# A pool of their own for the staging tiles of q, and the normalising multiply placed between the mask multiplies on VectorE

## The chip, the cores and the metric

The kernel runs on one core of a Trainium2 chip. The metric is the device time of one execution in microseconds (us), lower is better; here the executions of one kernel within one set of rounds lie within 0.26% of each other. TensorE is called PE in the profile (PEld is its weight load), VectorE DVE, ScalarE ACT, GpSimd POOL, and SyncE, which issues the DMA transfers here, SP. A "verdict" of faster or slower takes 2%.

## The reference

Two layers, each an attention block and a token-mixing MLP, with a layer norm and a residual sum around each. Only the attention matters here: every query looks at 8 keys, at distances 0, 2, ..., 14.

```python
def _A_ref(x, wqkv, wo):                      # x: 1 x 2048 x 1024, bf16
    H = 32; Dh = D // H; W, dil = 8, 2
    q, k, v = ...                             # x @ wqkv, 32 heads of 32
    idx = pos[:, None] - (jnp.arange(W) * dil)[None, :]
    mask = idx >= 0
    logits = einsum("bhsd,bhswd->bhsw", q, k[idx]) * scale
    attn = softmax(where(mask, logits, -1e9))
    return einsum("bhsw,bhswd->bhsd", attn, v[idx]).reshape(B, S, D) @ wo
x = x + _A_ref(layernorm(x), A_wqkv, A_wo)
x = x + _B_ref(layernorm(x), ...)             # MLP over the tokens, 2048 -> 3584 -> 2048
# the same two lines once more
```

## The kernel before

The attention runs in 32 *visits* per layer. A visit computes scores of four heads for half of the even or of the odd tokens (512 queries), then the values of the visit before it, then two 512-column pieces of the next q or k projection. Even visits (b = 0) project q, odd visits (b = 1) project k. The parts that the change touches:

```python
x2p = pool("x2p", 6)      # six tiles in turn: residual loads xr, sums xn, reciprocals rd, q staging qs (and others)
pcp = pool("pcp", 2)
psa = pool("psa", 1, space=bass.MemoryType.PSUM)     # acc: ONE buffer
# ...
def qk_chunk(u, wts, part, n):                # 8 matmuls into ps
    # ...
    if part:
        nc.scalar.copy(out=kT[u % 2][:, ls], in_=ps[:])
    else:
        qs = x2("qs", [P, 512])
        nc.scalar.copy(out=qs[:], in_=ps[:])
        for h in range(HG):                   # 4 q copies, 32 partitions each: head h from partition 32*h
            hp = slice(h * DH, (h + 1) * DH)
            nc.vector.tensor_copy(out=qB[u % 2][hp, h, ls], in_=qs[hp, :])

def scores(u, b):
    # ... 16 matmuls into ss
    nc.scalar.activation(out=pc[:]..., in_=ss[...], func=ACT.Exp, ...)
    for r in range(P // KG):                  # masks 0, 1, 2, 3: 32 partitions each, mask r from partition 32*r
        rp = slice(r * KG, (r + 1) * KG)
        nc.vector.tensor_tensor(out=Pm[rp, ...], in0=pc[rp], in1=mk, op=ALU.mult)

def values(u, b, v, oT):
    acc = a_tile()
    # if b: 4 tiny matmuls on the block before (8 columns)      -> "values, first line" (L404)
    # 16 matmuls on this block: need all four masks             -> "values, second line" (L408)
    # matmuls with ones: the sums of the softmax
    nc.scalar.activation(out=rd[:], in_=acc[:, 1, :], func=ACT.Ln)
    nc.scalar.activation(out=rd[:], in_=rd[:], func=ACT.Exp, scale=-1.0)
    nc.vector.tensor_tensor(out=oT[g][...], in0=acc[:, 0, :], in1=rd[:], op=ALU.mult)   # "normalise"

def out_proj(c, i, oT, wo, res, dst, h2):
    xr = x2("xr")
    nc.sync.dma_start(out=xr[:], in_=res(c, i))                    # residual load
    # per half: 8 matmuls, then xn = ps + xr on VectorE, which frees the PSUM tile ps
    nc.sync.dma_start(out=rows(dst, c, i), in_=xn[:])              # store
    # ...

for vis in range(2 * NU):
    # ...
    in_order(scores, u, b)
    if vis:
        in_order(values, *divmod(vis - 1, 2), v, oT)
    for n in range(2):
        if u + 1 < NU:
            in_order(qk_chunk, u + 1, wts, *chunks[2 * b + n])
        else:
            in_order(out_proj, 0, 2 * b + n, oT, wo, res, xa[li], h2)
```

The first line of values runs only for b = 1, that is, in the *even* visit that follows.

The softmax here doesn't subtract the row's maximum and nothing guards it: scores larger than these inputs give would overflow.

## Time and profile before

| | before |
|---|---|
| time, median (range) | 1304.88 us (1304.62 to 1305.46, 3 runs); 1305.1 us with the 3 runs beside the changed kernel |
| span of the profiled run | 1303.6 us, granted clock 1.00 |
| PE, DVE, ACT busy | 98%, 35%, 29% |
| PE idle behind the residual add | 7.3 us |

From the page: the line of busy times (microseconds, share of the span, instructions), then the chain of waits that ended last, as shares of the span by engine.

```profile
PE 1278.7 (98%) x8258; PEld 592.9 (45%) x8414; DVE 454.4 (35%) x971; ACT 372.4 (29%) x628; POOL 2.4 (0%) x15
...
PE 95%; DMA 2%; DVE 2%; issue 1%; ACT 1%; DVEq 0%; SPq 0%
```

TensorE bounds the kernel, and VectorE is hardly on the chain. The waits view for PE (who waited for whom: total us, times, longest):

```profile
PE m L448 <- DVE xn L450: 7.3, 6, 2.0
PE m L352 <- issue: 4.6, 29, 0.2
```

The second line needs no cause: some matmul records are missing from the trace (963 of 1024 in this group).

The timeline of one pair of visits in layer 1. Columns: start, duration (of the whole merged group), engine, line, operation, out<-in, shapes, count, and in brackets the idle time ahead of it. L380 is scores, L383 the exponential, L388 the masks, L425 the end of the reciprocal, L427 the normalise, L362 the q copies, L404 and L408 the values.

```profile
152.58 0.46 PE L380 MATMUL s<-qB,kT 128*32 128x160 bf16 x16
...
154.00 2.02 DVE L388 TENSOR_TENSOR Pm<-pc,band 32x640 bf16<-32x640 bf16 x4 [1.14 <-ACT pc L383]
154.48 0.63 ACT L425 ACTIVATE rd<-rd 128x512 f32<-128x512 f32 x1
...
156.06 0.69 DVE L427 TENSOR_TENSOR oT<-acc,rd 128x512 bf16<-128x512 f32 x1
156.66 2.38 DVE L362 COPY qB<-qs 32x512 bf16<-32x512 bf16 x8
...
157.07 0.46 PE L380 MATMUL s<-qB,kT 128*32 128x160 bf16 x16
...
157.36 0.41 PE L408 MATMUL acc<-Pm,v 128*32 128x136 bf16 x16
...
159.07 2.03 DVE L388 TENSOR_TENSOR Pm<-pc,band 32x640 bf16<-32x640 bf16 x4
...
161.13 0.69 DVE L427 TENSOR_TENSOR oT<-acc,rd 128x512 bf16<-128x512 f32 x1
...
161.48 0.46 PE L380 MATMUL s<-qB,kT 128*32 128x160 bf16 x16
...
161.88 0.19 PE L404 MATMUL acc<-Pm,v 128*32 128x8 bf16 x4
...
161.90 0.42 PE L408 MATMUL acc<-Pm,v 128*32 128x136 bf16 x16
```

Two things are to be seen. First, VectorE works with gaps of 0.05 us at most from 154.00 to 161.82 (161.13 + 0.69), 7.82 us of the 8.90 us between the two even visits. Second, PE waits for the end of that chain although no idle time is listed. In the odd visit values start 0.29 us after the scores (157.36 - 157.07); in the even visit they start 0.40 us after (161.88 - 161.48), which is 0.06 us after the normalise ended. Recorded matmuls overlap: in the odd visit the scores end at 157.53, 0.17 us after the start of values. In the even visit their recorded end, 161.94, is 0.06 us after the start of values, and so it covers the wait.

### The profile page before, as it was taken

Reading aid. Unit: us, or ns where it says so; the run is one execution under the profiler, and the core shown is the slowest. Engines: PE = TensorE matmul, PEld = TensorE weight load, DVE = VectorE, ACT = ScalarE, POOL = GpSimd, SP = SyncE. Lnnn points to the kernel's source line nnn. Section 1 sums busy time; section 2 is a strip of 40 time slices with the busy share of each in tenths; the row PEclk is TensorE's granted clock in tenths of the full one; section 3 lists DMA queues with packets and bytes.
Section 4 is the critical chain, followed back from the end, with each engine's and each line's share of the span. In section 5 each row is a group of like instructions: output and inputs, shape, how many; then the busy total and the mean of one; then the engine's idle time right before and its main releaser. Section 6 shows DMA issues by size and latency. Waiting matters only on the chain.

```text
span 1303.6 us, 19189 instructions
## 1 busy us (share of the span) xinstructions
PE 1278.7 (98%) x8258; PEld 592.9 (45%) x8414; DVE 454.4 (35%) x971; ACT 372.4 (29%) x628; POOL 2.4 (0%) x15
## 2 busy tenths in 40 slices
PE   9999999999999999999999999999999999999998
PEld 4444444444444444444444444444444444444443
DVE  7468888820000013322300788888000000111111
ACT  5356665431111110000023666654211111000000
POOL 0000000000000000000000000000000000000000
PEclk9999999999999999999999999999999999999999
DMA  8620113452223236465432101034522222334330
GB/s 236 134 76 18 34 34 105 139 154 82 80 65 88 60 94 153 123 153 146 129 81 64 35 23 29 18 130 155 145 65 81 81 60 73 109 105 137 113 92 32
DMA packets 195812, 121.58 MB, mean 93 GB/s; under 512 B 37904, under 2 KB 177424, under 8 KB 195728
## 3 DMA queue, kind: packets, MB, share of 16 engines
q1 hardware_dynamic: 195728, 120.36, 32.6%
q8 instruction: 65, 1.06, 0.3%
q14 instruction: 19, 0.16, 0.0%
HBM read 96.48 MB, written 16.78 MB: 87 GB/s over the span
## 4 chain that ended last, share of the span: by engine, by line
PE 95%; DMA 2%; DVE 2%; issue 1%; ACT 1%; DVEq 0%; SPq 0%
PE m L352 17%; PE s L518 15%; PE s L475 15%; PE acc L475 7%; PE m L475 7%; PE m L518 7%; PE acc L518 7%; PE m L448 6%; PE m L337 4%; PE m L255 4%; PE s L380 2%; PE acc L408 1%; DMA xr<-in_A_x_dram 1%; PE acc L412 1%; DMA xr<-xb 1%
## 5 line engine op out<-in xcount | busy, mean ns | idle before, releaser
L518 PEld LDWEIGHTS <-w 128*128 128x128 bf16 x1792 | 175.3, 98 | 211.4
L475 PEld LDWEIGHTS <-w 128*128 128x128 bf16 x1792 | 175.3, 98 | 211.4
L352 PE MATMUL m<-hT,wqk 128*128 128x512 bf16 x963 | 223.4, 379 | 6.2 <-issue 4.6
L521 DVE SCALAR_TENSOR_TENSOR xo<-s,b_sb,xs 128x512 bf16<-128x512 f32 x32 | 24.0, 751 | 539.8 <-PE s L518 533.5
L475 PE MATMUL s<-h,w 128*128 128x512 bf16 x878 | 201.3, 379 | 0.8
L518 PE MATMUL s<-g,w 128*128 128x512 bf16 x884 | 199.3, 379 | 0.7
L352 PEld LDWEIGHTS <-wqk 128*128 128x128 bf16 x1024 | 95.2, 98 | 118.0 <-issue 10.7
L388 DVE TENSOR_TENSOR Pm<-pc,band 32x640 bf16<-32x640 bf16 x256 | 123.7, 483 | 46.0 <-ACT pc L383 39.2
L448 PE MATMUL m<-wo,oT 128*128 128x512 bf16 x500 | 111.9, 379 | 7.9 <-DVE xn L450 7.3
L475 PE MATMUL acc<-h,w 128*128 128x512 bf16 x440 | 103.1, 379 | 0.5
L518 PE MATMUL acc<-g,w 128*128 128x512 bf16 x436 | 99.7, 379 | 0.5
L362 DVE COPY qB<-qs 32x512 bf16<-32x512 bf16 x256 | 72.6, 284 | 77.5 <-ACT qs L359 73.4
L475 PE MATMUL m<-h,w 128*128 128x512 bf16 x438 | 98.5, 379 | 0.5
L518 PE MATMUL m<-g,w 128*128 128x512 bf16 x436 | 98.3, 379 | 0.6
L174 ACT ACTIVATE ln<-mv,eps 128x1 f32<-128x1 f32 x64 | 18.9, 295 | 244.2 <-DVE mv L182 238.8
L448 PEld LDWEIGHTS <-oT 128*128 128x128 bf16 x512 | 49.6, 98 | 68.6 <-issue 10.3
L482 ACT ACTIVATE g<-s,b_sb 128x1024 bf16<-128x1024 f32 x28 | 31.2, 1113 | 166.1 <-PE s L475 154.3
L255 PE MATMUL m<-wv,hT 128*128 128x512 bf16 x250 | 55.6, 379 | 1.0 <-ACT hT L249 0.7
L337 PE MATMUL m<-wv,hT 128*128 128x512 bf16 x251 | 55.2, 379 | 0.3
L359 ACT CAST qs<-m 128x512 bf16<-128x512 f32 x64 | 37.5, 585 | 51.4 <-PE m L352 50.3
L383 ACT ACTIVATE pc<-s,shift 128x640 bf16<-128x640 f32 x64 | 51.1, 799 | 0.0
L356 ACT CAST kT<-m 128x512 bf16<-128x512 f32 x64 | 37.5, 585 | 46.5 <-PE m L352 46.5
(57 smaller groups left out, 677.3 us busy)
## 6 DMA issues: line engine op xcount, KB each, us to landing
w<-in_B_w_dram SPq DMA_DIRECT2D x56, 512.0 KB, 3.8
w<-in_B_w_dram SPq DMA_DIRECT2D x64, 448.0 KB, 4.6
wqk<-in_A_wqkv_dram SPq DMA_DIRECT2D x16, 512.0 KB, 5.7
xa<-xn SPq DMA_DIRECT2D x32, 256.0 KB, 2.0
xs<-xa SPq DMA_DIRECT2D x32, 256.0 KB, 3.3
wv<-in_A_wqkv_dram SPq DMA_DIRECT2D x8, 512.0 KB, 5.2
wo<-in_A_wo_dram SPq DMA_DIRECT2D x8, 512.0 KB, 4.0
xr<-in_A_x_dram SPq DMA_DIRECT2D x16, 256.0 KB, 3.2
```

The costliest lines, as they stand in the source:

```text
L255: r = nc.tensor.matmul(pss_[k, n][:], lhsT=hT[:, kt, cols(*order[k])], rhs=wv[n][kt // 4][:, kt % 4, :], start=(kt == 0), stop=(kt == KD - 1))
L337: nc.tensor.matmul(ps[:], lhsT=hT[:, kt, cols(c, i)], rhs=wv[n][kt // 4][:, kt % 4, :], start=(kt == 0), stop=(kt == KD - 1))
L352: mm = nc.tensor.matmul(ps[:], lhsT=wts[part][:, kt, (g % 2) * P:(g % 2 + 1) * P], rhs=hT[:, kt, lo:lo + 512], start=(kt == 0), stop=(kt = ...
L356: nc.scalar.copy(out=kT[u % 2][:, ls], in_=ps[:])
L359: nc.scalar.copy(out=qs[:], in_=ps[:])
L362: nc.vector.tensor_copy(out=qB[u % 2][hp, h, ls], in_=qs[hp, :])
L383: nc.scalar.activation(out=pc[:].rearrange("p (n t) h k -> p n (t h k)", n=2), in_=ss[:, :, 0:2 * HG * GW], func=ACT.Exp, scale=scale, bia ...
L388: nc.vector.tensor_tensor(out=Pm[rp, :, s0:s0 + HB, r * KG:r * KG + GW].rearrange("p h t k -> p t h k"), in0=pc[rp], in1=mk, op=ALU.mult)
L448: mm = nc.tensor.matmul(ps[:], lhsT=oT[g][:, cols(c, i)], rhs=wo[n][g // 4][:, g % 4, :], start=(g == 0), stop=(g == NG - 1))
L475: nc.tensor.matmul(pairs[fl][0][dc], lhsT=wt[c][:, i, fl * P:(fl + 1) * P], rhs=h2[c][i][:, dc * 512:(dc + 1) * 512], start=(k == 0), stop ...
L482: nc.scalar.activation(out=g[fb][:, fl, :].rearrange("p (n d) -> p n d", n=2), in_=t[:], func=ACT.Gelu_apprx_tanh, bias=b1_sb[:, ft:ft + 1])
L518: nc.tensor.matmul(aps[dc], lhsT=w2t[ft // HF][:, ft % HF, c::DIL], rhs=g[ft // GF][:, ft % GF, dc * 512:(dc + 1) * 512], start=(ft == 0), ...
```

## The change

There are two intents. With the q staging tiles in a pool of their own, the residual loads need not wait for them. And if the normalise comes ahead of masks 2 and 3, the single acc buffer is free about 1 us earlier for the next values.

```diff
+    qsp = pool("qsp", 2)
 ...
-            qs = x2("qs", [P, 512])
+            qs = qsp.tile([P, 512], BF16, name="qs", tag="qs")
 ...                                      # scores(): the mask loop becomes a function
-        for r in range(P // KG):
+        masks.append((pc, s0))
+        return mm
+    masks = []
+    def mask(rs):
+        pc, s0 = masks[-1]
+        for r in rs:
 ...
-        nc.vector.tensor_tensor(out=oT[g][...], in0=acc[:, 0, :], in1=rd[:], op=ALU.mult)
+        chain_("DVE", lambda: nc.vector.tensor_tensor(out=oT[g][...], in0=acc[:, 0, :], in1=rd[:], op=ALU.mult))
 ...
             in_order(scores, u, b)
+            chain_("DVE", mask, (0, 1))
             if vis:
                 in_order(values, *divmod(vis - 1, 2), v, oT)
+            chain_("DVE", mask, (2, 3))
```

`chain_("DVE", ...)` fixes the order of these instructions on VectorE. The order of the built instructions confirms it: masks 0 and 1, normalise, masks 2 and 3, then the q copies. ScalarE's and SyncE's orders are unchanged. On PE a few matmuls of the first MLP product move into the last visits of each layer.

More of the change, by code (lines that the diff above doesn't have):

```diff
@@ L384, in scores @@
                              func=ACT.Exp, scale=scale, bias=shift[:])
-        for r in range(P // KG):
+        masks.append((pc, s0))
[4 more added lines that the diff above has]
+        for r in rs:
             rp = slice(r * KG, (r + 1) * KG)
             mk = band[rp].unsqueeze(1).unsqueeze(1).to_broadcast([KG, HB, HG, GW])
-            nc.vector.tensor_tensor(out=Pm[rp, :, s0:s0 + HB, r * KG:r * KG + GW].rearrange("p h t k -> p t h k"),
+            mm = nc.vector.tensor_tensor(out=Pm[rp, :, s0:s0 + HB, r * KG:r * KG + GW].rearrange("p h t k -> p t h k"),
                                     in0=pc[rp], in1=mk, op=ALU.mult)
@@ L426, in values @@
         lo = c * SC + t0 * P
-        nc.vector.tensor_tensor(out=oT[g][:, lo:lo + HB * P], in0=acc[:, 0, :], in1=rd[:], op=ALU.mult)
+        chain_("DVE", lambda: nc.vector.tensor_tensor(out=oT[g][:, lo:lo + HB * P], in0=acc[:, 0, :], in1=rd[:], op=ALU.mult))
         return mm
```

## The prediction

> **What bounds the kernel now.** TensorE. Busy table: PE 1278.7 of 1303.6 us (98%), VectorE 35%, ScalarE 29%; chain of waits: 95% PE. The waits view leaves PE only 7.3 us behind the residual add (xn, line 450, six waits, longest 2.0 us) and 4.6 us of "issue". No change of VectorE order can reach 2%.
>
> PE's busy share hides one more wait. [...] In the timelines of both attention stages (from 72 and 727 us) the first values matmul of every even visit (line 404, needs the single acc buffer) starts 0.06 us after the normalising multiply (line 427) ends: 0.33 to 0.42 us after that visit's scores begin, against 0.28 in odd visits. Unlisted, PE waits here some 0.05 to 0.14 us, about 30 times: 2.5 us in all. The cause is a VectorE chain: four mask multiplies 2.03 us, normalise 0.69, eight q copies 2.38, four masks 2.03, normalise 0.69: 7.8 us of each 8.95 us pair of visits, begun only when the exponentials land, 1.42 us after the scores.
>
> **What the change does.** No work is added or removed.
>
> 1. Own pool for qs. The residual loads do not move: the instruction orders show the SyncE order unchanged, and the first two loads stand behind a first-MLP weight load released by the last q/k projection (issued 206.8 us, used 211.3). Worth 0.
> 2. Normalise after masks 0 and 1. acc comes free one microsecond earlier, which helps line 404 alone (four tiny matmuls). The next values matmuls (line 408) need all four masks, and masks 2 and 3 now end where the normalise ended: the same VectorE work stands ahead of PE. In even visits the reciprocal is ready 2.53 us after the scores and two masks end at 2.42, so VectorE stalls about 0.14 us, newly. Against it, whatever follows the normalise starts about 0.09 us before its recorded end, so ending on masks may give 0.1 back. The wait and the period share a delay, so 0.14 us costs some 0.06 per pair: 0 to +1.7 us over 30 pairs; I take +0.9.
> 3. In each layer's last visits the PE order shifts: two matmuls of the first MLP product (0.45 us) go ahead of the residual-add wait that lasted 1.10 us, into idle time; but two residual adds come before their statistics, which delays the next tile's add and its load by about 0.25. Net -0.2 to -0.4 us per layer, -0.6 in all.
>
> **Predicted time: 1305.2 us**, 8 in 10 between 1303.0 and 1307.4. Faster by over 2%: 0.005; within 2%: 0.985; slower by over 2%: 0.01.
>
> **What would show it.** Step 1: residual loads issue at the same distance from the last scores. Step 2: in even visits line 404 starts 0.28 us after the scores, but line 408 still late, at 0.38 to 0.46, about 0.06 us after the last mask; a VectorE gap before the normalise of about 0.1 us; the pair of visits 8.95 to 9.01 us. Step 3: two first-product matmuls ahead of a wait cut from 1.1 to about 0.6 us.
>
> **What would make it wrong.** If the mask that follows the normalise overlaps it by more than I read, or masks run faster when not back to back, the chain shortens and PE gains up to 2.5 us. [...] If an earlier load after all moves, up to 7 us of residual-add waits could go.

1304.9 us before, 0 for the pool, +0.9 for VectorE's order and -0.6 for the last visits come to 1305.2 us.

## The result, and the profile after

The changed kernel takes 1307.95 us (median of 6 runs, 1307.27 to 1309.03) against 1305.1 us (6 runs, 1304.62 to 1306.53). The ratio is 1.0022, with a 95% interval of 1.0009 to 1.0035. Ratios are the mean time of one kernel's runs over that of the other's of the same rounds, so they are not quite the ratio of the quoted medians. The change costs 0.2%: within 2% of before, but above the predicted range, which ended at 1307.4 us.

The page's lines of busy times and of the chain:

```profile
PE 1280.4 (98%) x8258; PEld 593.9 (45%) x8414; DVE 457.0 (35%) x971; ACT 373.0 (29%) x628; POOL 2.4 (0%) x15
...
PE 87%; DVE 6%; ACT 3%; DMA 1%; issue 1%; SPq 0%; DVEq 0%
```

The busy shares are the same. But PE's share of the chain fell from 95% to 87%, and DVE and ACT came in: VectorE's chain now shows in the listing too. The waits view of PE:

```profile
PE m L456 <- DVE xn L458: 5.4, 6, 1.3
...
PE acc L416 <- DVE Pm L396: 0.5, 2, 0.3
```

The wait behind the residual add fell by 1.9 us, and a new one appeared: values (now L416) behind a mask (now L396). The timeline of the pair that answers to the one above (scores L381, masks L396, reciprocal L433, normalise L435, q copies L363, values L412 and L416):

```profile
153.83 0.46 PE L381 MATMUL s<-qB,kT 128*32 128x160 bf16 x16
...
155.25 0.99 DVE L396 TENSOR_TENSOR Pm<-pc,band 32x640 bf16<-32x640 bf16 x2 [1.02 <-ACT pc L384]
155.74 0.63 ACT L433 ACTIVATE rd<-rd 128x512 f32<-128x512 f32 x1
156.40 0.69 DVE L435 TENSOR_TENSOR oT<-acc,rd 128x512 bf16<-128x512 f32 x1 [0.16 <-ACT rd L433]
...
157.12 1.00 DVE L396 TENSOR_TENSOR Pm<-pc,band 32x640 bf16<-32x640 bf16 x2
158.16 2.38 DVE L363 COPY qB<-qs 32x512 bf16<-32x512 bf16 x8
...
160.57 0.99 DVE L396 TENSOR_TENSOR Pm<-pc,band 32x640 bf16<-32x640 bf16 x2
...
161.59 0.69 DVE L435 TENSOR_TENSOR oT<-acc,rd 128x512 bf16<-128x512 f32 x1
162.32 1.00 DVE L396 TENSOR_TENSOR Pm<-pc,band 32x640 bf16<-32x640 bf16 x2
...
162.83 0.46 PE L381 MATMUL s<-qB,kT 128*32 128x160 bf16 x16
...
163.12 0.18 PE L412 MATMUL acc<-Pm,v 128*32 128x8 bf16 x4
...
163.37 0.42 PE L416 MATMUL acc<-Pm,v 128*32 128x136 bf16 x16
```

The first line of values (L412) no longer waits: 0.29 us after the scores. The second (L416) waits longer: 0.54 us after them. VectorE's chain runs from 155.25 to 163.32, 8.07 us instead of 7.82. The extra 0.25 us has two parts:

- The stall for the reciprocal: the normalise starts 0.16 us after mask 1 ended. Before, it started 0.03 us after mask 3. That is 0.13 us (about 0.14 us on average over the pairs).
- The seams around the normalise in the even visit (a seam is where one instruction follows the other on the engine): before, the q copy started at 156.66, 0.09 us *before* the normalise's end at 156.75. Now mask 2 starts at 157.12, 0.03 us *after* its end at 157.09. That is 0.12 us.

Taken apart by the starts of scores in the two traces, the span of the changed kernel grew by 0.35 us up to the first even visit (start-up: 72.58 and 72.93 us; in five other traces it lies between 72.55 and 73.36). It grew by 1.58 us in the 14 pairs of layer 1, shrank by 1.06 us from there to layer 2, grew by 1.54 us in its 13 pairs, and shrank by 0.61 us to the end: together +1.8 us, the difference of the spans (1305.4 - 1303.6). The two medians differ by 2.85 us; the profiled run of before was one of its slower ones (it took 1305.6 us, against the median of 1305.1).

### The profile page after: what moved, and what is told of

It is laid out like the page before. It is cut to its first block, busy times and chain, and to the rows that moved or that the text cites. A ratio compares the mean times of both kernels' runs of the same rounds, so it can differ in the third digit from the quotient of the medians.

```text
span 1305.4 us, 19220 instructions
## 1 busy us (share of the span) xinstructions
PE 1280.4 (98%) x8258; PEld 593.9 (45%) x8414; DVE 457.0 (35%) x971; ACT 373.0 (29%) x628; POOL 2.4 (0%) x15
## 3 DMA queue, kind: packets, MB, share of 16 engines
q8 instruction: 65, 1.06, 0.3%
## 4 chain that ended last, share of the span: by engine, by line
PE 87%; DVE 6%; ACT 3%; DMA 1%; issue 1%; SPq 0%; DVEq 0%
PE s L526 15%; PE s L483 15%; PE m L353 11%; PE acc L526 7%; PE m L526 7%; PE m L483 7%; PE acc L483 7%; PE m L456 7%; PE m L338 4%; PE m L256 4%; DVE Pm L396 3%; DVE qB L363 2%; DVE oT L435 1%; PE acc L416 1%; PE s L381 1%
## 5 line engine op out<-in xcount | busy, mean ns | idle before, releaser
L396 DVE TENSOR_TENSOR Pm<-pc,band 32x640 bf16<-32x640 bf16 x256 | 123.6, 483 | 42.3 <-ACT pc L384 35.6
L363 DVE COPY qB<-qs 32x512 bf16<-32x512 bf16 x256 | 72.8, 285 | 78.3 <-ACT qs L360 73.3
```

Source lines behind the costliest of these rows:

```text
L396: mm = nc.vector.tensor_tensor(out=Pm[rp, :, s0:s0 + HB, r * KG:r * KG + GW].rearrange("p h t k -> p t h k"), in0=pc[rp], in1=mk, op=ALU.mult)
```

## The experiments

Each kernel was run in 5 rounds, with runs of the kernel before on the same chip. All results were correct. "Pair" is the mean distance between the scores of even visits in layer 1 and layer 2 of its trace, without the start of the attention: the first pair of each layer is shorter (8.36 us; its first visit has no values to compute), and in layer 2 the second is left out too. "Wait" is how long after the scores the second line of values starts in even visits, on average over both layers. "Chain" is VectorE's chain in one pair, where it was read.

| kernel | median us | before, same rounds | ratio (95%) | pair, layer 1 / 2 | wait | chain |
|---|---|---|---|---|---|---|
| before | | | | 8.949 / 8.955 | 0.39 | 7.82 |
| changed | 1307.95 | 1305.1 | 1.0022 (1.0009 to 1.0035) | 9.061 / 9.073 | 0.50 | 8.07 |
| pool_only | 1305.45 | 1304.61 | 1.0006 (0.9993 to 1.0018) | 8.946 / 8.947 | 0.39 | |
| order_only | 1307.34 | 1304.61 | 1.0021 (1.0008 to 1.0033) | 9.061 / 9.076 | 0.51 | |
| even_only | 1308.23 | 1304.61 | 1.0031 (1.0017 to 1.0044) | 9.071 / 9.082 | 0.52 | |
| odd_only | 1304.08 | 1304.61 | 0.9999 (0.9986 to 1.0011) | 8.934 / 8.936 | 0.37 | |
| three_even | 1307.60 | 1304.96 | 1.0014 (1.0001 to 1.0028) | 9.011 / 9.016 | 0.45 | 7.96 |
| dup_mask | 1313.02 | 1304.96 | 1.0064 (1.0051 to 1.0076) | 9.211 / 9.211 | 0.66 | 8.36 |
| pool2 | 1307.03 | 1304.96 | 1.0013 (1.0000 to 1.0025) | 8.951 / 8.940 | 0.39 | |
| odd_pool2 | 1307.25 | 1304.96 | 1.0014 (1.0001 to 1.0026) | 8.968 / 8.957 | 0.41 | |
| early_xr | 1303.42 | 1305.25 | 0.9985 (0.9972 to 0.9999) | 8.949 / 8.952 | 0.39 | |
| early_xr_odd | 1302.71 | 1305.25 | 0.9981 (0.9969 to 0.9994) | 8.937 / 8.939 | 0.38 | |
| early_defer_odd | 1299.90 | 1305.25 | 0.9958 (0.9946 to 0.9971) | 8.937 / 8.940 | 0.38 | |
| zero_last_even | 1303.44 | 1304.83 | 0.9991 (0.9979 to 1.0004) | 8.881 / 8.877 | 0.32 | 7.68 |
| snake | 1303.68 | 1304.83 | 0.9986 (0.9972 to 1.0000) | 8.862 / 8.863 | 0.32 | 7.60 |
| early_defer_odd_snake | 1297.84 | 1304.83 | 0.9947 (0.9934 to 0.9959) | 8.860 / 8.860 | 0.32 | 7.60 |

### Which half of the change costs the time: pool_only, order_only

```diff
 # pool_only: before, and only
+    qsp = pool("qsp", 2)
-            qs = x2("qs", [P, 512])
+            qs = qsp.tile([P, 512], BF16, name="qs", tag="qs")
 # order_only: the changed kernel without these lines
```

> The kernel before with only the own pool for the q staging tiles; its TensorE, VectorE and SyncE orders are those of before. Theory (the order of VectorE's work makes the loss): 1305.1 us, within 0.5 us of before, pair of visits 8.95 us. Rival (the pool makes the loss, through the added wait of ScalarE's q copy for VectorE): 1308 us, pair 9.06 us.

> The changed kernel with the q staging tiles back in the pool of the residual loads: only the VectorE order changes (and the TensorE order of the last visits with it). Theory: as the changed kernel, about 1308 us, pair of visits 9.06 us. Rival (the pool makes the loss): 1305 us, pair 8.95 us.

The order alone reproduces the loss (ratio 1.0021; pair 9.061 us, as in the changed kernel). The pool alone leaves the pair where it was, and the time is not told apart from before. So the loss comes from VectorE's order.

### Which place costs it: even_only, odd_only

```diff
-            chain_("DVE", mask, (0, 1))
+            chain_("DVE", mask, (0, 1) if b == 0 else (0, 1, 2, 3))      # even_only; odd_only has b == 1
             if vis:
                 in_order(values, *divmod(vis - 1, 2), v, oT)
-            chain_("DVE", mask, (2, 3))
+            if b == 0:                                                   # odd_only: b == 1
+                chain_("DVE", mask, (2, 3))
```

> Own pool, and the normalise between the masks in even visits only (those that copy q); odd visits as before. Theory: the VectorE chain grows by the stall for the reciprocal (0.13 us) and by the lost overlap of the copy with the end of the normalise (0.12 us), 0.25 us together, and half of it shows: pair 9.07 us, and, as the TensorE order of the last visits is that of before, about 1308.6 us. Rival (each place costs its share): pair 9.00 us, 1306.7 us.

> Own pool, and the normalise between the masks in odd visits only; even visits as before. Theory: there the reciprocal is ready in time and no copy follows the normalise, so the chain keeps its length within 0.03 us: pair 8.94 to 8.97 us, 1304.3 to 1305.5 us. Rival (each place costs its share): pair 9.00 us, 1306.7 us.

The even visits carry all of the loss: pair 9.07 us as expected. In odd visits, where the reciprocal is ready in time and no q copy follows the normalise, the same order even gains a little: 0.01 us per pair against pool_only, which differs from it in the order alone. The medians of even_only and of the whole change are not told apart (their intervals overlap). In the traces even_only is 1.1 us longer, and 0.94 us of it lie between the pairs of layer 1 and those of layer 2, a stretch in which PE's order is that of before; that this order is the cause is not shown.

### How a longer chain becomes time: dup_mask

```diff
 # before, and
-        for r in range(P // KG):
+        for r in [0, 1, 2, 3] + ([3] if b == 0 else []):
```

> The kernel before with the last mask multiply of every even visit done twice (same result), 0.51 us more in the VectorE chain. Theory (the delay is shared between the wait and the period, half shows): pair 9.20 us, 1312 us. Rival 1 (VectorE at 35% has slack): 8.95 us, 1304.8 us. Rival 2 (the delay shows in full): pair 9.46 us, 1320 us.

The trace of VectorE shows that the repeated mask was placed behind the normalise:

```profile
157.97 0.69 DVE L427 TENSOR_TENSOR oT<-acc,rd 128x512 bf16<-128x512 f32 x1
158.69 0.49 DVE L388 TENSOR_TENSOR Pm<-pc,band 32x640 bf16<-32x640 bf16 x1
159.21 2.39 DVE L362 COPY qB<-qs 32x512 bf16<-32x512 bf16 x8
```

With the seams, the chain grew by 0.54 us (7.82 to 8.36). The pair grew by 0.26 us, half of it; both rivals fail. The reason is a feedback. Call T the pair's length, T0 its length without the wait, w the wait, C the time from the scores of one even visit until the chain that they start lets the values of the next even visit run, and f the part of it (0.29 us) that passes before values could start anyway. Then w = C - T - f, and the period is T = T0 + w. Put together, T = (T0 + C - f) / 2: a chain longer by x lengthens the period by x/2, because the wait also postpones the scores that start the next chain. The trace of before shows this visit by visit: a long wait makes the next one short. From the fourth even visit of layer 1 on, the first line of values starts 0.32, 0.40, 0.33, 0.38, 0.35 and 0.38 us after the scores, and each two neighbours add up to 0.71 to 0.73 us. With VectorE busy 35% of the span, an extra half microsecond every 9 us still cost 8 us in all.

### The stall or the seams: three_even

```diff
-            chain_("DVE", mask, (0, 1))
+            chain_("DVE", mask, (0, 1, 2) if b == 0 else (0, 1, 2, 3))
 ...
-            chain_("DVE", mask, (2, 3))
+            if b == 0:
+                chain_("DVE", mask, (3,))
```

> Own pool; in even visits the normalise stands after three masks instead of two, so the reciprocal is ready in time (no stall), but a mask still follows the normalise and the q copies follow a mask; odd visits as before. Theory: only the lost overlap of 0.12 us is left in the chain, half shows: pair 9.01 us, 1306.6 us. Rival (the stall for the reciprocal is all of the loss): pair 8.95 us, 1304.8 us.

Timeline of VectorE in one pair of three_even:

```profile
155.22 1.51 DVE L396 TENSOR_TENSOR Pm<-pc,band 32x640 bf16<-32x640 bf16 x3 [1.15 <-ACT pc L384]
156.76 0.69 DVE L435 TENSOR_TENSOR oT<-acc,rd 128x512 bf16<-128x512 f32 x1
157.48 0.49 DVE L396 TENSOR_TENSOR Pm<-pc,band 32x640 bf16<-32x640 bf16 x1
158.00 2.39 DVE L363 COPY qB<-qs 32x512 bf16<-32x512 bf16 x8
```

The stall is gone (the normalise follows the mask after 0.03 us). The mask still starts 0.03 us after the normalise's end (157.45), and the copy 0.03 us after the mask's (157.97). The pair is 9.01 us, so a bit more than half of the loss stays without any stall. Both parts are real, and about equally large.

### Why a mask does not overlap the end of the normalise: zero_last_even, snake

In the trace of before, only one kind of seam between masks, normalise and q copies overlaps: q copy 0 starts 0.08 to 0.09 us before the end of the normalise ahead of it, at all 28 places where it follows without a wait. It is also the only one at which both instructions start in the same partitions (from partition 0). At all others (a mask or a q copy and the next one, mask 3 and the normalise, the last q copy and mask 0) the partitions change, and where nothing is waited for, the next starts 0.01 to 0.03 us after the end. In the changed kernel mask 2, from partition 64, follows the normalise, and it starts 0.03 us after. The start partitions would explain the seams (theory A), but so would "a mask never overlaps" (theory B). Two kernels tell them apart.

```diff
 # zero_last_even: as three_even, but
+            chain_("DVE", mask, (1, 2, 3) if b == 0 else (0, 1, 2, 3))
 ...
+                chain_("DVE", mask, (0,))
 # snake: before, and the second four q copies backwards
-            for h in range(HG):
+            for h in range(HG) if n == 0 else reversed(range(HG)):
```

> As the run with three masks ahead of the normalise in even visits, but the masks ahead are 1, 2 and 3 and the one behind is mask 0, which starts at partition 0 as the normalise and the first q copy do. Theory A [...]: the mask starts 0.08 us before the end of the normalise, the q copy before the end of the mask; the chain is some 0.1 us shorter than before, pair 8.90 us, about 1303.5 us. Theory B (a mask never overlaps the end of the instruction ahead, whatever its partitions): gaps of 0.03 us, pair 9.01 us, about 1307 us.

> The kernel before with one edit: the second four of the eight q copies go through the heads backwards (3, 2, 1, 0), so that copy 3 follows copy 3 and mask 0 follows copy 0, with no change of partitions at these two places. Theory A: mask 0 starts 0.08 us before the end of the last copy instead of 0.03 us after it, the chain shortens by 0.11 to 0.2 us, half shows: pair 8.87 to 8.89 us, about 1302.8 us. Theory B: nothing moves, 8.95 us, 1305 us.

VectorE in one pair of zero_last_even:

```profile
155.65 0.69 DVE L435 TENSOR_TENSOR oT<-acc,rd 128x512 bf16<-128x512 f32 x1
156.26 0.47 DVE L396 TENSOR_TENSOR Pm<-pc,band 32x640 bf16<-32x640 bf16 x1
156.66 2.44 DVE L363 COPY qB<-qs 32x512 bf16<-32x512 bf16 x8
```

and of snake:

```profile
156.65 2.27 DVE L362 COPY qB<-qs 32x512 bf16<-32x512 bf16 x8
158.85 2.02 DVE L388 TENSOR_TENSOR Pm<-pc,band 32x640 bf16<-32x640 bf16 x4
...
161.42 0.46 PE L380 MATMUL s<-qB,kT 128*32 128x160 bf16 x16
...
161.71 0.18 PE L404 MATMUL acc<-Pm,v 128*32 128x8 bf16 x4
```

Mask 0 starts 0.08 us before the normalise's end (156.34), and the copy 0.07 us before the mask's end (156.73). In snake, mask 0 starts 0.07 us before the last copy's end (158.92); before, it started 0.03 us after it (156.66 + 2.38 = 159.04, then 159.07). So at these seams a mask does overlap when it starts in the same partitions as the instruction ahead, and that is worth 0.10 to 0.11 us for each. In zero_last_even the mask behind the normalise also lost a wait for an old semaphore value, and several other seams shrank from 0.03 to 0.01 us (the normalise starts at 155.65, mask 3 ended at 155.64), where a semaphore wait or update had gone as well; so not all of the 0.14 us by which its chain is shorter is due to the partitions. Whether the semaphores made those seams shrink was not tested. snake has no such difference at its seam, so it is the cleaner proof. The expected pairs were 8.90 and 8.87 to 8.89; the traces have 8.88 and 8.86.

In snake the first line of values starts 0.29 us after the scores (161.71 - 161.42), as in odd visits, and the second 0.32 us after them, in all even visits but one per layer. So PE waits no more: 8.86 us is the pair without the wait. Before lost (8.95 - 8.86) x 27 = 2.4 us to it. The median of snake, 1303.68 us, is only 1.2 us below that of before in the same rounds. Its interval ends at 1.0000, so by the clock alone the gain is hardly told from nothing; the trace's pairs are what shows it. In that trace the stretch behind the pairs of layer 2 is 1.35 us longer than in before (453.31 against 451.96 us), which takes back half of the gain; why was not looked into.

### Less work on VectorE instead: pool2, odd_pool2

```diff
 # pool2: before; odd_pool2: odd_only
-                nc.vector.tensor_copy(out=qB[u % 2][hp, h, ls], in_=qs[hp, :])
+                (nc.gpsimd if h == 3 else nc.vector).tensor_copy(out=qB[u % 2][hp, h, ls], in_=qs[hp, :])
```

> The kernel before with two of the eight q copies of a pair on the idle GpSimd engine: 0.59 us less in the VectorE chain, more than twice the mean wait of TensorE (0.09 us). Theory: the values matmuls of even visits start 0.28 to 0.30 us after the scores, the pair falls to 8.86 us, about 1302.2 us. Rivals: GpSimd's copies slow VectorE down or come late, pair 8.95 us or more, 1305 us or more; or the waits that the timeline suggests are not real and nothing moves, 1304.8 us.

> The last two of use together: normalise between the masks in odd visits only, own pool, and two of eight q copies on GpSimd. Theory: no wait of TensorE is left in the pair for either order, so the same as with the copies alone within 0.5 us: pair 8.85 us, about 1302 us, and any order of VectorE serves. Rival: the order still counts, and this is 0.5 us or more below.

Both miss: the pair stayed at 8.94 to 8.97 us, and the time rose by 2 us. The timeline of pool2 shows why the chain did not shorten:

```profile
156.66 0.87 DVE L362 COPY qB<-qs 32x512 bf16<-32x512 bf16 x3
...
157.19 0.58 ACT L359 CAST qs<-m 128x512 bf16<-128x512 f32 x1 [1.14 <-PE m L352]
...
157.81 1.21 DVE L362 COPY qB<-qs 32x512 bf16<-32x512 bf16 x3 [0.29 <-ACT qs L359]
...
157.91 0.67 POOL L362 COPY qB<-qs 32x512 bf16<-32x512 bf16 x1 [1.18 <-ACT qs L359]
```

After the first three copies VectorE waits for ScalarE's second cast (0.29 us), which lands 0.68 us after the odd visit's scores; in before it landed 0.69 us after them in every pair. The three copies that then run beside GpSimd's take 1.21 us, as long as four take alone (half of the eight in before, 1.19 us). Taken singly, the loss lies in one of them: in nearly every pair the second of the three, which overlaps GpSimd's copy, takes 0.61 us and ends 0.15 us after it, while the two others keep their 0.28 us. The first three copies, which GpSimd's copy overlaps for only 0.06 us (156.66 to 156.72), take 0.87 us. Why the one copy beside GpSimd's is slow was not shown. The wait (0.29 us) and the slow copy (0.33 us) make up for the 0.59 us that were taken off VectorE. The theory left out both; the first rival had named GpSimd's slowing.

The extra 2 us come from elsewhere, from the first residual load of layer 1. It landed late in both traces of this kind (5.9 and 5.6 us from its issue to the add, against 4.2 to 4.7 in the other traces that issue it there); why, stays open. PE then waited 2.68 us in pool2, and its clock fell from 1.00 ahead of the wait to 0.50 behind it. The windows view of pool2: window, length, busy times of PE, PEld, DVE, ACT and POOL with counts, then the granted clock, DMA share and GB/s:

```profile
209.00:210.50 1.50, 1.50 (x9) 0.69 (x7) 1.28 (x3) 0.00 (x0) 0.00 (x0) 1.00 1.10 358
...
215.00:216.00 1.00, 1.00 (x4) 0.37 (x3) 0.63 (x2) 0.29 (x1) 0.00 (x0) 0.50 0.43 168
```

The 16 matmuls behind the wait took 5.30 us (5.25 in odd_pool2, where the clock was 0.50 too, after a wait of 2.33 us), against 3.61 in before, where the first wait was 1.31 us. In pool2 the mean granted clock is back at 0.93 from 216.90 to 218.00 us. In before the longest wait, the third, was 1.98 us (from 229.43 to 231.41 us), and the granted clock behind it stayed at 1.00. These traces do not show more about what lowers the clock.

### Why the pool moved no load, and a version that beats both: early_xr, early_xr_odd, early_defer_odd, early_defer_odd_snake

In these traces SyncE issues in the order of its program. In the trace of before it stood for 30.9 us at a weight load of the first MLP product, which waits for the last q projection to free its tile. The first two residual loads stood behind it and a second such load, and were issued from 206.80 us on. early_xr has the own pool of the change and moves these loads forward in the program; early_xr_odd does so on odd_only. early_defer_odd, also on odd_only, chains SyncE's order as well, so that each store of a sum comes after the residual load of the tile two later.

```diff
+            if vis == 2 * NU - 4:                       # the first two residual loads, four visits before the end
+                for k in range(2):
+                    pre[order[k]] = load_xr(*order[k], res)
 ...                                                     # out_proj:
-        xr = x2("xr")
-        nc.sync.dma_start(out=xr[:], in_=res(c, i))
+        xr = pre.pop((c, i), None) or load_xr(c, i, res)
 ...                                                     # early_defer_odd (loads are chained on SP too):
-        nc.sync.dma_start(out=rows(dst, c, i), in_=xn[:])
+        late.append((rows(dst, c, i), xn))
+        while len(late) > (2 if (c, i) != order[-1] else 0):
+            to, t = late.pop(0)
+            chain_("SP", lambda: nc.sync.dma_start(out=to, in_=t[:]))
```

> Own pool for the q staging tiles, VectorE order of before, and the first two residual loads of each layer allocated four visits before the end of the attention, so that they stand ahead of the last weight load of the first MLP product in SyncE's order. Theory (the pool alone does nothing because the loads stand behind that weight load): they issue some 4 us earlier, the first wait of TensorE for the residual add falls from 1.3 us to 0.3 us or less in each layer, about 1303.0 us. Rival (the loads are late for want of a free tile): they issue where they did, and nothing moves, 1305 us.

> The same early residual loads with the normalise between the masks in odd visits only. Theory: the gains of the two add, 1302.6 us. Rival: no better than the early loads alone.

> The same again, and each store of a residual sum issued after the residual load of the tile two later, so that loads no longer stand behind stores. Theory: the second and third waits for the residual add (1.1 and 2.0 us in each layer) fall too, all waits for it together from 7 us to 2 us or less, about 1300 us. Rival: the waits turn into others (VectorE, tile reuse), 1302 us or more.

> The best version so far (early residual loads, stores behind loads, normalise between the masks in odd visits only) with the backward order of the second four q copies. Theory A: the gains add, pair 8.86 us, about 1297.7 us. Theory B: 1299.9 us as without it.

SyncE in the trace of before, then of early_xr (start and duration of merged issues):

```profile
201.91 4.78 SPq L463 DMA_DIRECT2D w<-in_B_w_dram  x2
206.80 1.38 SPq L442 DMA_DIRECT2D xr<-in_A_x_dram  x2
```

```profile
174.69 5.42 SPq L445 DMA_DIRECT2D xr<-in_A_x_dram  x2
201.96 0.38 SPq L470 DMA_DIRECT2D w<-in_B_w_dram  x1
```

The first load is issued 32 us earlier, the second 28 (I had expected 4). PE's first wait behind the residual add falls from 1.31 us in layer 1 and 1.35 in layer 2 to 0.25 in both. The rival, want of a free tile, is out: pool_only has the same pools, and its loads were issued as late as those of before (0.58 us after the scores of the last pair in both). Whether the early loads need the pool of their own was not tested; every version with them has it. early_xr_odd (1302.71 us) is not told apart from early_xr (1303.42 us) by the clock; its pair is 0.012 us shorter. PE's waits in early_defer_odd:

```profile
PE m L462 <- DVE xn L464: 2.3, 4, 0.9
```

That is 2.3 us instead of 7.3 (a little above the 2 that I had expected), with the time at 1299.90 us, as expected. With the backward copies added it is 1297.84 us, 0.5% below the kernel before. The gains add, as expected (the two versions ran in different rounds: 0.9947 against 0.9958 of before).

## Why the prediction was wrong

- *What bounds the kernel* (PE, with a hidden wait at the end of VectorE's chain): right. snake, which only shortens the chain, takes the wait away, and dup_mask lengthens it.
- *Step 1, the pool is worth 0*: right, and for the reason given. pool_only leaves the order and the pair unchanged; the loads move when they are put ahead of the weight load.
- *Step 2, the mechanism*: right. The first line of values starts 0.29 us after the scores, the second one late and just behind the last mask, and half of the chain's growth shows.
- *Step 2, the size*: wrong, and here the prediction failed. It put the stall at 0.14 us (measured 0.13) and went on: "whatever follows the normalise starts about 0.09 us before its recorded end, so ending on masks may give 0.1 back". That was read at one seam, the normalise followed by a q copy. Mask 2 starts 0.03 us *after* the normalise's end, and the q copy, now behind a mask, lost its overlap. Instead of 0.1 us given back, 0.12 us more were lost. The chain grew by 0.25 us and the pair by 0.11 (predicted 0 to 0.06). Over 27 pairs this is 3.1 us in the traces, where the sum had +0.9. three_even shows this part alone, and zero_last_even and snake show that it goes with the partitions in which the next instruction starts (0.07 to 0.08 us before the end in the same ones, 0.03 us after it in others). The text named a loss of 2 to 4 us for masks behind the normalise among what would make it wrong, but its sum (0 to +1.7 us) left it out.
- *Step 3, the last visits*: its order of PE is right, its size stays open. The two matmuls did move ahead of the second wait for the residual add, but that wait fell from 1.10 to 0.87 us in layer 1, not to 0.6; the third, ahead of which two more had moved, fell from 1.98 to 1.28. All waits together fell from 7.3 to 5.4 us (order_only has 5.6; the seven traces with before's PE order there have 6.4 to 7.3), so the sign fits. The sum had -0.6 us; the stretches behind the pairs are 1.06 and 0.61 us shorter than in before. But in those seven traces they scatter by 0.9 and 1.8 us (510.91 to 511.84 and 451.50 to 453.31 us), and the changed kernel and order_only lie only just below (510.69 and 451.33, 510.86 and 451.40). How much of the gain is the moved matmuls, and how much the landing times of loads, was not separated.
- *Within 2%*: right. But the interval of the ratio is clear of 1: the change makes the kernel slower by 0.1% to 0.35%.

## What to carry to other kernels

An engine that is busy a third of the time can still bound a loop: add up its chain from the event that starts it to the event that waits for it, and when the wait also delays the next start, expect half of any change of the chain to show (dup_mask: 0.54 us in the chain, 0.26 us in the pair). Before an instruction is moved, look at its seams, not only at its duration: in these traces a mask or a q copy (32 partitions) started 0.07 to 0.09 us before the end of the one ahead when both start in the same partitions, and 0.01 to 0.03 us after it when they don't and nothing else is waited for. Reversing one loop over heads was worth as much as the whole hidden wait in the trace (0.09 us per pair). The pool of its own moved no load here (pool_only). If a load stands behind a blocked one in its queue, move it in the queue: early_xr issued its first load 32 us earlier.
